# Loading w_in through GpSimd's DMA queue and a q sketch in eight tiles, in a fused sketched-attention and feed-forward kernel

## Chip, cores and metric

The kernel runs on one core of a Trainium2 chip. The metric is the device time of one execution in microseconds (us); where several executions were timed, their median.

## What is computed

Polynomial-sketch attention over 4 batches and 4 heads (1088 positions, head size 32), then a feed-forward layer with a squared ReLU over all 4352 tokens:

```python
def phi(x):
    a = np.einsum('rd,bhsd->bhsr', S1, x)      # r = 8
    b = np.einsum('rd,bhsd->bhsr', S2, x)
    return np.einsum('bhsi,bhsj->bhsij', a, b).reshape(*x.shape[:-1], r * r)
q_p, k_p = phi(q), phi(k)
kv = np.einsum('bhsf,bhsd->bhfd', k_p, v)
z = np.sum(k_p, axis=2)
num = np.einsum('bhsf,bhfd->bhsd', q_p, kv)
den = np.einsum('bhsf,bhf->bhs', q_p, z)[..., None] + 1e-06
x = (num / den).transpose(0, 2, 1, 3).reshape(B * S, H * D)
out = np.maximum(x @ w_in, 0.0) ** 2 @ w_out   # w_in 128 x 2048, w_out 2048 x 128
```

## The kernel before

The feed-forward layer is cut into ten chunks of tokens (256 to 512 columns, `FC`) and each chunk into 16 blocks of 128 hidden columns. One unit is one or two blocks: a matmul of w_in's block with xT (`ffn1`, L597), ReLU (L609 on ScalarE, or L607 on VectorE), square (L620 or L622), and a matmul with w_out's block that adds up in `po` (`ffn2`, L641). w_in's matmuls run on the type float32r, so w_in is loaded as float32 into `w_in32` (`load_wi`, L208, four quarters of 512 columns) and cast by GpSimd into `w_in` (`cast_wi`, L685). The attention of batches 1 to 3 is woven into the feed-forward work by a planner (`_Order`), which lays out all later instructions by estimated costs and due times; the change leaves it as it is.

What the change touches is the prologue, written out by hand, which brings the first 256 columns of xT for batch 0. In order:

- Loads. S1 and a first piece of v (64 KB, token tiles 0 to 3 of partition group 0) go out on ScalarE's queue; S2, two pieces of k, the first 256 columns of q, seven more pieces of v, then w_in and w_out quarters, more q and the next batches go out on SP's queue, one after another (L181 to L213).
- While k is on its way TensorE runs fillers (`keep_warm`, L692) and the little product that spreads S1 and S2 (`sp`, L703; copied to `ss` by ScalarE, L706). GpSimd builds `iden` and `sel`, then from `ss` the q sketch weights `sq` (L721), the replicator `irep` (L728), pads and small weights (L732 to L744).
- k: VectorE transposes k in four groups of token tiles, (0,2), (2,2), (4,3), (7,2) (`a_kT0`, L290); TensorE sketches each token tile with four 128x32 matmuls (`a_kf`, L315); ScalarE copies one half to `kb` (L321); VectorE multiplies the halves to `kp` (`a_kp0`, L331); TensorE adds kp with v and a column of ones to `kvp` (`a_kv0`, L396).
- q: VectorE transposes 256 columns (`a_qT`, L296), TensorE sketches them (`q0`, L756, four matmuls on 64x128 tiles), ScalarE copies one half (`qb0`, L767), VectorE multiplies (`qp0`, L774).
- Then numerator, denominator and normalization: `zb`, `bd`, `zm` on VectorE (L789 to L800), `den` and `num` on TensorE (L816, L821), transposes and a reciprocal on VectorE (L837 to L843), and the product into xT (L844). ScalarE copies kvt and sw (L809, L830), TensorE replicates kvt (L440). One filler (L835) already reads w_in; then the first L597.

An engine works through its instructions in the order written. In `kernel` order TensorE sees all four `a_kf`, both `q0`, then all `a_kv0`; VectorE sees the four `a_kT0`, `a_qT`, then the four `a_kp0`. `kvp` takes a buffer that the second `a_kf` has used, so it follows the second `a_kp0`.

Of the kernel before, what the change touches and what calls it, by code (L numbers as in the profile page):

```python
# [10 lines left out]
F32R = mybir.dt.float32r  # L11
# [3 lines left out]
def _ap(t: bass.AP, p0: int, np_: int, off: int, free):  # L15
    p = list(t.ap)[0]
    return bass.AP(
        t.tensor, t.offset + p0 * p[0] + off, [[p[0], np_]] + [list(d) for d in free]
    )
# [88 lines left out]
def kernel(  # L108
# [11 lines left out]
    nc = tc.nc  # L120

    B, H, S, D = 4, 4, 1088, 32
# [5 lines left out]
    GT, G2, LA = 4, 6, 3.5  # L128
    LU = 4
    KC = [(0, 160), (160, 128)]  # L130
    W0, W1, W3 = 5, 3, 1
    ND, QT, WI, KL, QL = 2, 6.0, (1.0, 1.9), (30.0, 8.0), 4.0


# [10 lines left out]
    mult = mybir.AluOpType.mult  # L145
# [10 lines left out]
    psf = ctx.enter_context(tc.tile_pool(name="psf", bufs=2, space=bass.MemoryType.PSUM))  # L156
# [3 lines left out]
    def sb(name, cols, dt=F32, rows=128):  # L160
        return cpool.tile([rows, cols], dt, tag=name, name=name)
# [6 lines left out]
    vn = [sb("vn0", VC + 32), sb("vn1", VC)]  # L168
    kT, qT = sb("kT", SP), sb("qT", SP)
    xT = sb("xT", B * S + SP - S, F32R)  # L170
    w_in32, w_o, w_in = sb("w_in32", 2048), sb("w_o", 2048), sb("w_in", 2048, F32R)
    s_nat, ss, s2f = sb("s_nat", 32, rows=16), sb("ss", 80), sb("s2f", 32)
    sf, s_T = ss[:, 0:64], ss[:, 64:80]

# [22 lines left out]
    def load_v(eng, b, p, t0=0, t1=NT):  # L197
        n = 32 * ((t1 if p < 3 else min(t1, NT - 2)) - t0)
        eng.dma_start(
            _ap(vn[b % 2], 32 * p, 32, 32 * t0, [[32 * NT, H], [1, n]]),  # L200
            bass.AP(
                v.tensor, v.offset + b * H * S * D + 32 * first(b, t0, p),
                [[G * D, 32], [S * D, H], [1, n]],
            ),
        )

    def load_wi(eng, c):
        eng.dma_start(  # L208
            w_in32[:, 512 * c : 512 * c + 512], moe_w_in[:, 512 * c : 512 * c + 512]
        )  # L210

    def load_wo(eng, c):
        eng.dma_start(  # L213
            _ap(w_o, 0, 128, 512 * c, [[128, 4], [1, 128]]),
            bass.AP(
                moe_w_out.tensor, moe_w_out.offset + c * 512 * 128,
                [[128, 128], [128 * 128, 4], [1, 128]],
            ),
        )
# [2 lines left out]
    nc.sync.dma_start(s_nat[8:16, :], S2[:, :])  # L222
    load_k(nc.sync, 0, 0, 512)
    load_k(nc.sync, 0, 512, S)
    load_v(nc.scalar, 0, 0, 0, 4)
    load_q(nc.sync, 0, 0, 256)
    for t0, t1 in ((0, 4), (4, NT)):
        for p in range(0 if t0 else 1, 4):
            load_v(nc.sync, 0, p, t0, t1)

    zero_a = sb("zero_a", 8)
    nc.scalar.copy(zero_a[:, :], nc.const_aps.tensor(0.0, (128, 8), F32))

    sq, sel = sb("sq", 256), sb("sel", 320, rows=16)
    nc.vector.memset(sel[:, :], 0.0)
    nc.gpsimd.memset(_ap(vn[0], 96, 32, 32 * (NT - 2), [[32 * NT, H], [1, 64]]), 0.0)
    nc.gpsimd.memset(vn[0][:, VC : VC + 32], 1.0)
# [2 lines left out]
    kt0 = sb("kt0", SP)  # L240
# [8 lines left out]
    for i in range(2):  # L249
# [5 lines left out]
    own_h, own_q = sb("own_h", 4), sb("own_q", 2)  # L255
# [3 lines left out]
    nc.gpsimd.tensor_copy(  # L259
        _ap(sel, 0, 16, 64, [[80, 4], [1, 16]]), _ap(iden, 0, 16, 0, [[0, 4], [1, 16]])  # L260
    )
    nc.vector.tensor_reduce(
        out=own_h[:, :], in_=_ap(iden, 0, 128, 0, [[32, 4], [1, 32]]), op=add, axis=AX
    )
# [2 lines left out]
        out=own_f[:, :], in_=_ap(iden, 0, 128, 0, [[8, 16], [1, 8]]), op=add, axis=AX  # L267
# [11 lines left out]
    def banks(t_, x, col, n, k=2):  # L279

        return _ap(t_, 0, 128, 512 * x + col, [[512, k], [1, n]])
# [5 lines left out]
    def a_kT0(t0, n):  # L287
        p = 3 if t0 + n > NT - 2 else 4
        i = 32 * (first(0, t0, 1) - first(0, t0, 0))
        nc.vector.transpose(  # L290
            _ap(kt0, 0, 128, 128 * t0, [[32, p], [128, n], [1, 32]]),
            _ap(kn[0], 0, 128, 32 * first(0, t0, 0), [[i, p], [32, n], [1, 32]]),
        )

    def a_qT(b, i0, n):
        nc.vector.transpose(qT[:, 32 * i0 : 32 * i0 + 32 * n], qn[b % 2][:, 32 * i0 : 32 * i0 + 32 * n])  # L296
# [10 lines left out]
                )  # L307


    def a_kf(t0, n, pool, tag):  # L310
        kf = pool.tile([128, 512], F32, tag=tag, name="kf")
        for t in range(n):
            for c in range(4):
                o = 128 * (t0 + t) + 32 * c
                nc.tensor.matmul(  # L315
                    _ap(kf, 32 * c, 32, 32 * t, [[32 * n, 2], [1, 32]]),
                    kt0[:, o : o + 32],
                    sf,
                )
        kb = wpool.tile([128, 32 * 3], F32, tag="kb", bufs=4, name="kb")  # L320
        nc.scalar.copy(kb[:, 0 : 32 * n], kf[:, 32 * n : 64 * n])  # L321
        st["kf", t0] = kf, kb

    def new_kp(b):

        st[b, "kp"] = wpool.tile([128, 64 * NT * H], F32, tag="kp", name="kp")

    def a_kp0(t0, n):

        kf, kb = st["kf", t0]  # L330
        nc.vector.tensor_tensor(  # L331
            out=_ap(st[0, "kp"], 0, 128, 256 * t0, [[64, 4 * n], [8, 8], [1, 8]]),
            in0=_ap(kf, 0, 128, 0, [[8, 4 * n], [1, 8], [0, 8]]),
            in1=_ap(kb, 0, 128, 0, [[8, 4 * n], [0, 8], [1, 8]]),
            op=mult,
        )
# [344 lines left out]
        nc.vector.tensor_copy(ob[1][:, :], po[1][:, 0:128])  # L681
        store(1)

    def cast_wi(c):
        nc.gpsimd.tensor_copy(  # L685
            w_in[:, 512 * c : 512 * c + 512], w_in32[:, 512 * c : 512 * c + 512]
        )

    def keep_warm(n, cols=512):
        t_ = st["warm"]  # L690
        for _ in range(n):
            nc.tensor.matmul(  # L692
                t_[:, 0:cols],
                nc.const_aps.tensor(1.0, (128, 128), mybir.dt.bfloat16),
                nc.const_aps.tensor(1.0, (128, cols), mybir.dt.bfloat16),
            )
# [8 lines left out]
        )  # L705
    nc.scalar.copy(ss[:, :], sp[:, 0:80])  # L706
    load_q(nc.sync, 0, 256, 640)
    load_wi(nc.sync, 0)
    load_wi(nc.sync, 1)
    load_wi(nc.sync, 2)  # L710
    load_wo(nc.sync, 0)
    load_wo(nc.sync, 1)
    load_wi(nc.sync, 3)
    for c in range(2, 4):
        load_wo(nc.sync, c)
    load_q(nc.sync, 0, 640, S)
    keep_warm(W1)
    a_kT0(0, 2)
    a_kT0(2, 2)
    for x in range(2):  # L720
        nc.gpsimd.tensor_tensor(  # L721
            out=_ap(sq, 0, 128, 128 * x, [[64, 2], [8, 8], [1, 8]]),
            in0=_ap(ss, 0, 128, 72 - 8 * x, [[0, 2]] + [[[0, 8], [1, 8]], [[1, 8], [0, 8]]][x]),
            in1=_ap(own_q, 0, 128, 0, [[1, 2], [0, 8], [0, 8]]),
            op=mult,
        )
    for h in range(H):
        nc.gpsimd.tensor_copy(  # L728
            _ap(irep, 32 * h, 32, 0, [[32, 4], [1, 32]]),
            _ap(iden, 32 * h, 32, 32 * h, [[0, 4], [1, 32]]),  # L730
        )
    nc.gpsimd.memset(_ap(vn[1], 96, 32, 32 * (NT - 2), [[32 * NT, H], [1, 64]]), 0.0)  # L732
    for w in sw:
        nc.gpsimd.memset(w[:, 16:32], 0.0)
# [2 lines left out]
        out=_ap(sfk, 0, 128, 0, [[16, 2], [1, 16]]),  # L737
        in0=_ap(ss, 0, 128, 64, [[0, 2], [1, 16]]),
        in1=_ap(own_q, 0, 128, 0, [[1, 2], [0, 16]]),
        op=mult,  # L740
    )
    nc.gpsimd.memset(kT[:, S:SP], 0.0)
    nc.gpsimd.memset(qT[:, S:SP], 0.0)
    nc.gpsimd.memset(_ap(pd, 0, 128, 8, [[9, 4 * NT], [1, 1]]), 1e-6)  # L744

    a_kT0(4, 3)
    a_kT0(7, 2)
    a_qT(0, 0, 8)


    x0 = att("x0")

    def q0(x):
        for y in range(2):
            r, o = slice(64 * y, 64 * y + 64), 512 * (2 * x + y)
            nc.tensor.matmul(x0[:, o : o + 256], sq[r, 128 * x : 128 * x + 128], qT[r, 0:256])  # L756

    new_kp(0)
    qb0 = wpool.tile([128, 512], F32, tag="qb0", bufs=1, name="qb0")
    qp0 = wpool.tile([128, 512], F32, tag="qp0", bufs=1, name="qp0")  # L760
    a_kf(0, 2, psf, "po")
    a_kf(2, 2, psf, "pg")
    a_kf(4, 3, psf, "po")
    a_kf(7, 2, psf, "pg")
    q0(0)
    q0(1)
    nc.scalar.copy(_ap(qb0, 0, 128, 0, [[256, 2], [1, 256]]), banks(x0, 0, 0, 256))  # L767
    st[0, "kvp"] = psf.tile([128, 512], F32, tag="pg", name="kvp")
    for t0, n in ((0, 2), (2, 2), (4, 3), (7, 2)):
        a_kp0(t0, n)  # L770
        for t in range(t0, t0 + n):
            a_kv0(t)

    nc.vector.tensor_tensor(  # L774
        out=_ap(qp0, 0, 128, 0, [[256, 2], [1, 256]]), in0=banks(x0, 2, 0, 256),
        in1=_ap(qb0, 0, 128, 0, [[256, 2], [1, 256]]), op=mult,
# [7 lines left out]
    bd = sb("bd", 128)  # L784
    own = _ap(own_p, 0, 128, 0, [[0, 2], [1, 2], [0, 32]])

    for c in range(4):
        cast_wi(c)
    nc.vector.tensor_tensor(  # L789
        out=_ap(zb, 0, 128, 1, [[65, 2], [32, 2], [1, 1]]),  # L790
        in0=_ap(st[0, "kvp"], 0, 128, 32, [[64, 2], [0, 2], [1, 1]]),
        in1=_ap(own_p, 0, 128, 0, [[0, 2], [1, 2], [1, 1]]),
        op=mult,
    )
    nc.vector.tensor_tensor(
        out=_ap(bd, 0, 128, 0, [[64, 2], [32, 2], [1, 32]]),
        in0=_ap(st[0, "kvp"], 0, 128, 0, [[64, 2], [0, 2], [1, 32]]),
        in1=own, op=mult,
    )
    nc.vector.tensor_tensor(  # L800
        out=_ap(zm, 0, 128, 0, [[16, 2], [8, 2], [1, 8]]),
        in0=_ap(st[0, "kvp"], 0, 128, 32, [[64, 2], [0, 2], [1, 8]]),
        in1=_ap(own_f, 0, 128, 0, [[0, 2], [8, 2], [1, 8]]),
        op=mult,
# [46 lines left out]
    tu, t = [], 1.2  # L851
# [310 lines left out]
```

## Time and profile before

| | us |
|---|---|
| median of 3 runs | 184.5 (184.16 to 184.61) |
| profiled execution | 184.55 |
| its span, first to last instruction | 182.7 |
| TensorE busy in it | 178.3 |
| ScalarE, VectorE, GpSimd busy | 135.9, 121.8, 39.4 |
| first ffn1 matmul (L597) starts at | 12.95 |

Times in the timelines count from the start of the span. A line of a timeline reads: start, duration, engine, source line, operation, output<-inputs, tile shape on TensorE (rows*columns), operand shape, type, number of merged instructions; in brackets the idle time before it and what ended that. PE is TensorE, DVE VectorE, ACT ScalarE, POOL GpSimd, and a trailing q the DMA issues of an engine. A float32 matmul shows as two records, a float32r one as one. A matmul's duration includes its way through the array, so neighbours overlap; their pace is read from the distance of their starts.

### The profile page before, as it was taken

How to read it: one execution, taken by the hardware profiler on the slowest of the kernel's cores; microseconds unless marked ns; L12 is line 12 of the kernel's file. 1: busy time of each engine (PE TensorE's matmuls, PEld its weight loads, DVE VectorE, ACT ScalarE, POOL GpSimd, SP SyncE). 2: the span in 40 equal slices, each digit the busy share in tenths (PEclk: the TensorE clock that was granted, in tenths of full speed). 3: DMA queues.
4: the chain of work that ended last, by engine and by line, in shares of the span. 5: the costliest groups of instructions: out<-in, count | busy, mean ns of one | idle time of the engine just before them, and what ended most of it. 6: DMA issues, size and time to landing. Idle time of an engine off the chain costs nothing.

```text
span 182.7 us, 3995 instructions
## 1 busy us (share of the span) xinstructions
PE 178.3 (98%) x1529; PEld 105.3 (58%) x1529; DVE 121.8 (67%) x262; ACT 135.9 (74%) x258; POOL 39.4 (22%) x158
## 2 busy tenths in 40 slices
PE   8999999999999999999999999999999999999992
PEld 2768876755645655555455554545555554555792
DVE  3979969999999961799994335996353334333640
ACT  3329679849948886799937778894777777777990
POOL 5544418438300002570008100500000000000000
PEclk9999999999999999999999999999999999999999
DMA  5999990010029700000030200003003000300111
GB/s 150 225 304 341 298 238 17 4 32 0 0 47 238 179 0 4 4 2 0 0 54 14 43 0 5 0 0 59 0 4 57 0 0 5 52 0 0 32 29 29
DMA packets 24610, 11.26 MB, mean 62 GB/s; under 512 B 17936, under 2 KB 23056, under 8 KB 24592
## 3 DMA queue, kind: packets, MB, share of 16 engines
q1 hardware_dynamic: 24272, 10.89, 24.0%
q8 instruction: 12, 0.20, 0.4%
q10 hardware_dynamic: 320, 0.13, 0.3%
q14 instruction: 6, 0.05, 0.1%
HBM read 8.78 MB, written 2.23 MB: 60 GB/s over the span
## 4 chain that ended last, share of the span: by engine, by line
PE 98%; DVE 0%; issue 0%; ACT 0%; ACTq 0%
PE po L641 61%; PE pg L597 18%; PE nd L550 3%; PE po L636 2%; PE warm L692 2%; PE pol L636 2%; PE qc L303 2%; PE nd L414 1%; PE kvp L396 1%; PE kf L315 1%; PE qc L347 1%; PE kvp L414 1%; PE x L756 1%; PE nd L347 0%; PE den L816 0%; PE x L440 0%
## 5 line engine op out<-in xcount | busy, mean ns | idle before, releaser
L641 PE MATMUL po<-g,w_o 128*128 128x512 f32 (+3 forms) x288 | 122.7, 546 | 0.0
L609 ACT ACTIVATE gt<-pg 128x512 f32<-128x512 f32 (+3 forms) x144 | 75.2, 570 | 31.3 <-PE pg L597 30.8
L641 PEld LDWEIGHTS po<-g,w_o 128*128 128x128 f32 x288 | 53.4, 189 | 31.9 <-issue 24.8
L597 PE MATMUL pg<-xT,w_in 128*128 128x512 f32 (+3 forms) x160 | 70.2, 519 | 0.0
L620 ACT ACTIVATE g<-gt 128x512 f32<-128x512 f32 (+2 forms) x102 | 60.7, 623 | 1.6
L622 DVE TENSOR_TENSOR g<-gt 128x512 f32<-128x512 f32 (+3 forms) x43 | 30.0, 699 | 39.5 <-ACT gt L609 38.8
L597 PEld LDWEIGHTS pg<-xT,w_in 128*128 128x128 f32 x160 | 29.1, 190 | 28.6 <-ACT gt L609 11.5
L510 POOL COPY rd<-rc 32x9 f32<-32x9 f32 (+2 forms) x80 | 19.7, 246 | 26.5 <-DVE rc L502 23.3
L456 POOL COPY kv<-kvt 32x64 f32<-32x64 f32 x48 | 12.7, 264 | 44.7 <-DVE kvt L433 42.5
L519 DVE STREAM_SHUFFLE qa<-qc 128x576 f32<-128x576 f32 (+2 forms) x20 | 11.8, 647 | 0.0
L534 DVE TENSOR_TENSOR qp<-qa,qb 128x576 f32<-128x576 f32 (+2 forms) x20 | 10.8, 605 | 0.0
L482 DVE STREAM_TRANSPOSE qt<-qc 128x576 f32<-128x576 f32 (+2 forms) x10 | 5.8, 611 | 6.2 <-PE qc L347 4.4
L367 DVE TENSOR_TENSOR kp<-fs 128x576 f32<-128x576 f32 x12 | 8.7, 741 | 0.0
L645 DVE STREAM_TRANSPOSE oT<-po 128x512 f32<-128x512 f32 (+3 forms) x9 | 5.9, 653 | 2.1 <-PE po L641 2.1
L550 PE MATMUL nd<-qp,kv 32*32 32x288 f32 (+2 forms) x320 | 6.6, 354 | 0.0
L519 DVE STREAM_SHUFFLE qb<-qc 128x576 f32<-128x576 f32 (+2 forms) x10 | 6.1, 649 | 0.0
L567 DVE TENSOR_TENSOR xT<-nd,bc 128x576 fp32r<-128x576 f32 (+2 forms) x10 | 5.6, 594 | 0.6 <-PE nd L550 0.5
L636 PE MATMUL po<-w_o,g 128*128 128x128 f32 x32 | 5.8, 279 | 0.0
L296 DVE STREAM_TRANSPOSE qT<-qn 128x192 f32<-128x192 f32 (+3 forms) x11 | 5.8, 552 | 0.0
L636 PE MATMUL pol<-w_o,g 128*128 128x128 f32 x32 | 5.7, 275 | 0.0
L560 DVE STREAM_TRANSPOSE bc<-rd 128x576 f32<-128x576 f32 (+2 forms) x10 | 5.7, 596 | 0.0
L550 PEld LDWEIGHTS nd<-qp,kv 32*32 32x32 f32 x320 | 2.9, 103 | 3.6 <-issue 2.4
(106 smaller groups left out, 91.2 us busy)
## 6 DMA issues: line engine op xcount, KB each, us to landing
kn<-in_k_dram SPq DMA_DIRECT2D x3, 544.0 KB, 6.9
qn<-in_q_dram SPq DMA_DIRECT2D x3, 544.0 KB, 7.6
vn<-in_v_dram SPq DMA_DIRECT2D x9, 144.0 KB, 6.3
w_in<-in_moe_w_in_dram SPq DMA_DIRECT2D x4, 256.0 KB, 4.8
w_o<-in_moe_w_out_dram SPq DMA_DIRECT2D x4, 256.0 KB, 5.9
out_dram<-oT SPq DMA_DIRECT2D x12, 64.0 KB, 1.9
out_dram<-oT SPq DMA_DIRECT2D x8, 56.0 KB, 1.8
out_dram<-oT SPq DMA_DIRECT2D x8, 48.0 KB, 1.8
```

The source lines that it names most:

```text
L367: nc.vector.tensor_tensor(out=_ap(st[b, "kp"], 0, 128, 64 * NT * h, [[64, NT], [8, 8], [1, 8]]), in0=_ap(fs, 0, 128, o, [[32, NT], [1, 8], ...
L456: nc.gpsimd.tensor_copy(_ap(st[b, "kv"], 32 * c, 32, 64 * h, [[32, E], [1, 32]]), _ap(st["kvt"], 32 * h, 32, 0, [[64, E], [1, 32]]),)
L510: nc.gpsimd.tensor_copy(st[b, "rd", i0][32 * h : 32 * h + 32, n * c : n * c + n], st["rc"][32 * c : 32 * c + 32, n * h : n * h + n],)
L519: nc.vector.stream_shuffle(in_=banks(st[b, "qc", i0], 2 * x, 0, m), out=_ap(st[b, which, i0], 0, 128, 2 * m * x, [[m, 2], [1, m]]), mask=m ...
L534: nc.vector.tensor_tensor(out=st[b, "qp", i0, e][:, r], in0=st[b, f"qa{e}", i0][:, r], in1=st[b, "qb", i0][:, r], op=mult,)
L550: nc.tensor.matmul(nd[32 * h : 32 * h + 32, 512 * c : 512 * c + m], kv[r, o : o + 32], qp[r, m * h : m * h + m], start=(e == 0), stop=(e = ...
L597: nc.tensor.matmul(st["pg", u][:, n * i : n * i + n], w_in[:, 128 * (d0 + i) : 128 * (d0 + i) + 128], xT[:, c0 : c0 + n],)
L609: nc.scalar.activation(gt[:, 0:w], st["pg", u][:, 0:w], Relu)
L620: nc.scalar.activation(to, of, Square)
L622: nc.vector.tensor_tensor(out=to, in0=of, in1=of, op=mult)
L636: nc.tensor.matmul(po[x // 128][:, 0:128], g[:, x : x + 128], w, start=(d == 0), stop=(d == NB - 1),)
L641: nc.tensor.matmul(po[0][:, 0:n], w, g, start=(d == 0), stop=(d == NB - 1))
```

## The change

The first two pieces of v and all of w_in are issued by GpSimd. The load of w_in writes the float32r tile itself, so `w_in32` and the four casts are gone; two quarters go out behind the copies of `irep`, two behind the pads. SP issues w_out and q without w_in between. `sq` loses the multiplication by a mask, and the q sketch becomes eight matmuls on 32x64 tiles; its copy to `qb0` becomes two copies that each swap the partition halves. The first `a_kp0` now stands ahead of `a_qT` on VectorE; the last `a_kf` uses two 128x64 matmuls per token tile instead of four 128x32; of the three fillers after `sp` the last is 384 columns instead of 512.

```diff
-    W0, W1, W3 = 5, 3, 1
+    W0, W1, W3 = 5, 2, 1
...
-    def load_wi(eng, c):
-        eng.dma_start(
-            w_in32[:, 512 * c : 512 * c + 512], moe_w_in[:, 512 * c : 512 * c + 512]
+    def load_wi(c):
+        nc.gpsimd.dma_start(
+            w_in[:, 512 * c : 512 * c + 512], moe_w_in[:, 512 * c : 512 * c + 512]
         )
...
-    load_v(nc.scalar, 0, 0, 0, 4)
     load_q(nc.sync, 0, 0, 256)
     for t0, t1 in ((0, 4), (4, NT)):
-        for p in range(0 if t0 else 1, 4):
+        for p in range(0 if t0 else 2, 4):
             load_v(nc.sync, 0, p, t0, t1)
...
+    for p in range(2):
+        load_v(nc.gpsimd, 0, p, 0, 4)
...
-    def a_kf(t0, n, pool, tag):
+    def a_kf(t0, n, pool, tag, w=32):
         kf = pool.tile([128, 512], F32, tag=tag, name="kf")
         for t in range(n):
-            for c in range(4):
-                o = 128 * (t0 + t) + 32 * c
+            for c in range(0, 128, w):
+                o = 128 * (t0 + t) + c
                 nc.tensor.matmul(
-                    _ap(kf, 32 * c, 32, 32 * t, [[32 * n, 2], [1, 32]]),
-                    kt0[:, o : o + 32],
+                    _ap(kf, c, w, 32 * t, [[32 * n, 2], [1, 32]]),
+                    kt0[:, o : o + w],
                     sf,
                 )
...
     load_q(nc.sync, 0, 256, 640)
-    load_wi(nc.sync, 0)
-    load_wi(nc.sync, 1)
-    load_wi(nc.sync, 2)
-    load_wo(nc.sync, 0)
-    load_wo(nc.sync, 1)
-    load_wi(nc.sync, 3)
-    for c in range(2, 4):
+    for c in range(4):
         load_wo(nc.sync, c)
     load_q(nc.sync, 0, 640, S)
     keep_warm(W1)
+    keep_warm(1, 384)
...
     for x in range(2):
-        nc.gpsimd.tensor_tensor(
-            out=_ap(sq, 0, 128, 128 * x, [[64, 2], [8, 8], [1, 8]]),
-            in0=_ap(ss, 0, 128, 72 - 8 * x, [[0, 2]] + [[[0, 8], [1, 8]], [[1, 8], [0, 8]]][x]),
-            in1=_ap(own_q, 0, 128, 0, [[1, 2], [0, 8], [0, 8]]),
-            op=mult,
+        nc.gpsimd.tensor_copy(
+            _ap(sq, 0, 128, 64 * x, [[8, 8], [1, 8]]),
+            _ap(ss, 0, 128, 72 - 8 * x, [[[0, 8], [1, 8]], [[1, 8], [0, 8]]][x]),
         )
...
+    load_wi(0)
+    load_wi(1)
     nc.gpsimd.memset(_ap(vn[1], 96, 32, 32 * (NT - 2), [[32 * NT, H], [1, 64]]), 0.0)
...
     nc.gpsimd.memset(_ap(pd, 0, 128, 8, [[9, 4 * NT], [1, 1]]), 1e-6)
+    load_wi(2)
+    load_wi(3)
...
     a_kT0(7, 2)
-    a_qT(0, 0, 8)
...
     def q0(x):
-        for y in range(2):
-            r, o = slice(64 * y, 64 * y + 64), 512 * (2 * x + y)
-            nc.tensor.matmul(x0[:, o : o + 256], sq[r, 128 * x : 128 * x + 128], qT[r, 0:256])
+        for h in range(H):
+            r, o, p = slice(32 * h, 32 * h + 32), 512 * (2 * x + h // 2), 64 * ((h + 1 - x) % 2)
+            nc.tensor.matmul(
+                x0[p : p + 64, o : o + 256], sq[r, 64 * x : 64 * x + 64], qT[r, 0:256]
+            )
...
     a_kf(0, 2, psf, "po")
+    a_kp0(0, 2)
+    a_qT(0, 0, 8)
     a_kf(2, 2, psf, "pg")
     a_kf(4, 3, psf, "po")
-    a_kf(7, 2, psf, "pg")
+    a_kf(7, 2, psf, "pg", 64)
     q0(0)
     q0(1)
-    nc.scalar.copy(_ap(qb0, 0, 128, 0, [[256, 2], [1, 256]]), banks(x0, 0, 0, 256))
+    for i in range(2):
+        nc.scalar.copy(
+            _ap(qb0, 64 * i, 64, 0, [[256, 2], [1, 256]]),
+            _ap(x0, 64 - 64 * i, 64, 0, [[512, 2], [1, 256]]),
+        )
...
-    for c in range(4):
-        cast_wi(c)
```

More of the change, by code (lines that the diff above doesn't have):

```diff
@@ L170 @@
     xT = sb("xT", B * S + SP - S, F32R)
-    w_in32, w_o, w_in = sb("w_in32", 2048), sb("w_o", 2048), sb("w_in", 2048, F32R)
+    w_o, w_in = sb("w_o", 2048), sb("w_in", 2048, F32R)
     s_nat, ss, s2f = sb("s_nat", 32, rows=16), sb("ss", 80), sb("s2f", 32)
@@ L232 @@
     nc.scalar.copy(zero_a[:, :], nc.const_aps.tensor(0.0, (128, 8), F32))
-    sq, sel = sb("sq", 256), sb("sel", 320, rows=16)
+    sq, sel = sb("sq", 128), sb("sel", 320, rows=16)
     nc.vector.memset(sel[:, :], 0.0)
@@ L682, in f_last @@
         store(1)
[L684 to L687, printed above, removed]
     def keep_warm(n, cols=512):
@@ L744 @@
     nc.gpsimd.memset(_ap(pd, 0, 128, 8, [[9, 4 * NT], [1, 1]]), 1e-6)
+    load_wi(2)
+    load_wi(3)
     a_kT0(4, 3)
     a_kT0(7, 2)
-    a_qT(0, 0, 8)
     x0 = att("x0")
     def q0(x):
-        for y in range(2):
-            r, o = slice(64 * y, 64 * y + 64), 512 * (2 * x + y)
-            nc.tensor.matmul(x0[:, o : o + 256], sq[r, 128 * x : 128 * x + 128], qT[r, 0:256])
-    new_kp(0)
+        for h in range(H):
[3 more added lines that the diff above has]
+            )
     qb0 = wpool.tile([128, 512], F32, tag="qb0", bufs=1, name="qb0")
     qp0 = wpool.tile([128, 512], F32, tag="qp0", bufs=1, name="qp0")
+    new_kp(0)
     a_kf(0, 2, psf, "po")
+    a_kp0(0, 2)
+    a_qT(0, 0, 8)
     a_kf(2, 2, psf, "pg")
     a_kf(4, 3, psf, "po")
-    a_kf(7, 2, psf, "pg")
+    a_kf(7, 2, psf, "pg", 64)
     q0(0)
     q0(1)
-    nc.scalar.copy(_ap(qb0, 0, 128, 0, [[256, 2], [1, 256]]), banks(x0, 0, 0, 256))
+    for i in range(2):
[3 more added lines that the diff above has]
+        )
     st[0, "kvp"] = psf.tile([128, 512], F32, tag="pg", name="kvp")
     for t0, n in ((0, 2), (2, 2), (4, 3), (7, 2)):
-        a_kp0(t0, n)
+        if t0:
+            a_kp0(t0, n)
         for t in range(t0, t0 + n):
```

## The prediction

> **What bounds the kernel now.** I read the chain of the work that ended last first, then each engine's timeline over the first 18 us, then the waits of that stretch.
>
> ```profile
> PE 98%; DVE 0%; issue 0%; ACT 0%; ACTq 0%
> PE po L641 61%; PE pg L597 18%; PE nd L550 3%; PE po L636 2%; PE warm L692 2%; PE pol L636 2%; PE qc L303 2%; PE nd L414 1%; PE kvp L396 1%; PE kf L315 1%; PE qc L347 1%; PE kvp L414 1%; PE x L756 1%; PE nd L347 0%; PE den L816 0%; PE x L440 0%
> ```
>
> Almost everything is TensorE, most of it the feed-forward matmuls (L641, L597). From 15.9 us to the end they follow each other without a pause that another engine sets, and nothing in the change touches them. So only the stretch before can move the end, and it moves it one to one: what counts is when the first L597 starts (12.95 us) and how long the filling after it, 13 to 16 us, takes. TensorE's timeline there:
>
> ```profile
> 4.80 2.16 PE L315 MATMUL kf<-ss,kt 128*32 128x64 f32 x72
> 6.89 1.14 PE L756 MATMUL x<-qT,sq 64*128 64x256 f32 x8
> 7.96 2.32 PE L396 MATMUL kvp<-vn,kp 128*64 128x64 f32 x72
> ...
> 12.61 0.51 PE L835 MATMUL warm<-w_in 128*128 128x512 f32 x1
> 12.95 0.69 PE L597 MATMUL pg<-xT,w_in 128*128 128x256 f32 x4
> 13.57 0.45 PE L303 MATMUL qc<-qT,sw 32*32 32x96 f32 x32
> 14.01 0.47 PE L597 MATMUL pg<-xT,w_in 128*128 128x256 f32 x2
> ```
>
> L396 starts right behind the q sketch (L756) and runs at an even pace. VectorE shows what stands before and after:
>
> ```profile
> 4.20 0.77 DVE L290 STREAM_TRANSPOSE kt<-kn 128x256 f32<-128x256 f32 x2 [1.61 <-DMA kn<-in_k_dram]
> 5.17 0.84 DVE L290 STREAM_TRANSPOSE kt<-kn 128x384 f32<-128x384 f32 x2 [0.21 <-DMA kn<-in_k_dram]
> 5.94 0.40 DVE L296 STREAM_TRANSPOSE qT<-qn 128x256 f32<-128x256 f32 x1
> 6.26 2.71 DVE L331 TENSOR_TENSOR kp<-kf,kb 128x512 f32<-128x512 f32 x4
> 8.90 0.68 DVE L774 TENSOR_TENSOR qp<-x,qb 128x512 f32<-128x512 f32 x1
> 10.32 0.17 DVE L789 TENSOR_TENSOR zb<-kvp,own_p 128x4 f32<-128x4 f32 x1 [0.75 <-PE kvp L396]
> ```
>
> It waits twice: 0.21 us for the second piece of k, and 0.75 us for L396. So the path is: second piece of k, transposes, q sketch, kvp, then a fixed chain to xT and the first L597. GpSimd's casts, which vanish, look costly but are on no path:
>
> ```profile
> 10.70 0.61 POOL L685 CAST w_in<-w_in 128x512 fp32r<-128x512 f32 x1 [3.52 <-DMA w_in<-in_moe_w_in_dram]
> 11.65 1.26 POOL L685 CAST w_in<-w_in 128x512 fp32r<-128x512 f32 x2 [0.34 <-DMA w_in<-in_moe_w_in_dram]
> 15.00 0.61 POOL L685 CAST w_in<-w_in 128x512 fp32r<-128x512 f32 x1 [2.09 <-DMA w_in<-in_moe_w_in_dram]
> ```
>
> Quarters 0 to 3 of w_in are first used at 12.61, 14.01, 15.56 and 17.65 us (L597 runs through the 16 column blocks in order); the casts end at 11.31, 12.27, 12.91 and 15.61.
>
> **The change part by part.**
>
> *q sketch, later but shorter.* VectorE now does the first kp product before qT. That product takes a slot of 0.58 us (it starts at 6.26, the next at 6.84), so qT ends at 6.34 + 0.58 = 6.92 instead of 6.34; its place in the row of products is the same, so the later ones stay. TensorE sees a transpose 0.16 us after its end (first kt 4.64, first kf 4.80), so the sketch starts at 7.08 instead of 6.89: **+0.19**. Its length: before, 8 records on 64x128 tiles, two at a time, four rounds of 256 columns. Rounds start 0.21 us apart (7.21, 7.43, 7.64), that is 0.83 ns a column, so four rounds are 0.85 of the 1.14 us and 0.29 is start and drain. The nearest row with eight tiles is L347, 64x32, 32 records in 0.78 us: two rounds of 160 columns and two of 128 are 0.48, the rest 0.30. The same rest, so eight tiles do run at once. The new sketch has 16 records on eight tiles: two rounds, 0.43 + 0.30 = 0.73 us: **-0.41**. Together it ends 0.2 us earlier, and kvp with it: **-0.2**. Lower end: no eightfold overlap, -0 in length, so +0.19. Upper end: L396 can't start before the second kp product is read out of its buffer (ends 7.51, so 7.67 against 7.96): -0.29. I take -0.2, from the row that has the same number of tiles. Behind it the third product (8.38) must be there for kvp's record 32 (at 0.029 us each, 8.7 us) and the fourth (8.98) for record 56 (9.4 us); both are, barely.
>
> The Trainium skill (TensorEngine Tiling (Array Packing), Key Properties) says that tiles work independently, but that a change of the tiling mode drains the array, and the change adds one such switch by its 128x64 tiles in the last kf. By that rule the last kf's saving is eaten; the sum stays.
>
> *Last kf in 64-column tiles, 128 warm columns fewer.* Half the records (8 for 16), and a quarter of a 0.41 us filler. Both end before the sketch, which now waits for qT until 7.08 while kf is done by about 6.95: **0**, covered by that wait.
>
> *v's first two pieces to GpSimd.* The piece that ACT issued at 1.37 (64 KB, 3.1 us to landing) ran beside the two pieces of k (544 KB). At the 272 GB/s of the window 3.4 to 6.8 us, 64 KB are 0.24 us of all 16 engines. Gone from there, k's second piece lands up to 0.21 us earlier for VectorE (the idle time before 5.17), or not at all if GpSimd's pieces, issued at 2.4, come in just then. Ends 0 and -0.21; I take the middle, **-0.1**. The pieces themselves land by about 6.5 (2.4, two issues, 3.1 us), and kvp reads them at 7.7: cover 1.2 us.
>
> *qb0 in two copies on ACT.* 0.59 us each, from about 7.85: done at 9.05, so VectorE's qp0 starts 0.15 later than at 8.90 but has 0.75 us of idle time behind it: **0**.
>
> *sq as plain copies, casts gone.* sq is ready by 5 us, needed at 7.08: **0**. The last cast lies over VectorE's pd (L488, 0.59 us for 96 columns), which gets quicker by some 0.3 us (0.25 for 128 columns at 25.99), but TensorE never waits for that chain between 16 and 22 us: **0**.
>
> *w_in through GpSimd.* The trace has no DMA issue on GpSimd and none that converts. Its price on the engine, c: the nearest rows are ACT's issue, 0.35 us, and SP's, 0.43; the longest of SP's, 1.34, was held up by the queue. I take 0.5, near the undisturbed ones, and keep 1.34 for the range. Work between: sq and irep 1.9 us, the pads 1.4. Then the quarters are issued from 5.7, 6.2, 8.1 and 8.6 and land, at the 4.8 us of the old rows under load, at 10.5, 11.0, 12.9 and 13.4, against 12.3, 13.7, 15.3 and 17.3 needed (today's first uses less 0.3): **0**, cover 1.8 us or more. What queues behind on GpSimd: the pads of sw (read by ACT at 11.96) and the rd copies (16.42), both with 2 us to spare. SP loses five issues of 0.47 us, so w_o and the next batch come earlier; nobody waits for them: **0**.
>
> The Trainium skill (DMA: Bandwidth & Descriptors, Latency and other measured facts) puts the first byte at about 1 us for GpSimd's path and 0.6 for SP's and ACT's. With c = 1 the third quarter would land at 14.5 instead of 12.9: the sum would still be the same, with the cover down to 0.8 us.
>
> *Sum:* +0.19 - 0.41 - 0.1 = -0.3 us. The profiled execution took 184.55 us (span 182.7, 1.85 around it, which I leave), 0.05 above the median of 184.5; from the median the forecast is **184.2 us**.
>
> **The rivals.**
>
> *Everything that holds kvp goes.* The whole 0.21 of k, kvp at its earliest (7.67 - 0.21 = 7.46, against 7.96: -0.5), and 0.05 to 0.1 where VectorE's chain to xT no longer runs beside a cast (bc, L843, took 0.45 for 256 columns, qT 0.40). For it: VectorE and kvp are both tight, and both ends are given by rows. Against: all bounds must be met together. -0.6: **183.9**.
>
> *GpSimd's issue is dear (slower).* The third quarter lands at 10.5 + 4c (four issues, 2.4 start, 3.3 work, 4.8 landing; from c = 0.7 on GpSimd no longer waits for ss), needed at 15.3: it decides from c = 1.2 us. Above, L597 of column block 8 stalls and every 0.1 us of c costs 0.4; at 1.34 that leaves 184.8, at c = 1.6 it is 1.6 - 0.3 = 1.3 slower, **185.8**. A converting transfer that takes longer than 4.8 us under load does the same. For: no row of its price; against: all issue rows but the held-up ones are below 0.6.
>
> *It doesn't do what it says.* The sketch's tiles take turns and GpSimd's v pieces meet k's second piece: +0.19, **184.7**.
>
> *TensorE's clock steps up later.* Matmuls of kf start 27 ns apart at 4.8 us (16 in 0.40) and 14 ns apart at 6.7, so the array runs at half pace until about 6.5 although the page grants 1.0 throughout. If less filler let that step slip past kvp, its 72 records would take 53 ns each instead of 29: +1.7, with the sketch +2: **186.2**. Against: 0.1 us of filler in 6.
>
> The Trainium skill (TensorE: Matmul & The Clock Gate, Part 1) has the clock go up after one busy free-running window of about 3.4 us; that fits the step at 6.5, and by it a slip would cost one more such window.
>
> **How the numbers follow.** Forecast 0.48, everything goes 0.24, dear issue 0.17, tiles and v in the way 0.07, clock 0.04. About 0.3% (0.55 us) is what a measurement of this kernel can tell from no change. Only the second case passes it below (its sum -0.6, with a little from the forecast's upper end: 0.25); dear issue and clock pass it above, 0.21; the rest, 0.54, lies within. The range: below, 183.7 leaves out about 0.07 of the second case; above, 185.4 takes in the dear issue up to c = 1.5 and leaves out about 0.12. The likeliest case alone runs from 184.0 (both upper ends, -0.5) to 184.7 (+0.2).
>
> **What would show it.** L756 as 16 records on 32x64, starting near 7.1 and taking near 0.73; L396 starting near 7.65 instead of 7.96; VectorE's wait before the second kt group below 0.21; the first L597 near 12.65, and no wait of L835 or L597 for a DMA of w_in. On GpSimd, the gap of each DMA issue is c. It is wrong if L597 pauses at 14.0, 15.6 or 17.7, if kf or L396 run at twice their pace's spacing, or if the time around the span grows from 1.85 because a queue of another kind is in use.

## The result, and the profile after

The changed kernel takes 186.72 us in the median of 6 executions (185.47 to 188.06); the kernel before, on the same chip, 184.2. The ratio is 1.012, 95% interval 1.0083 to 1.0157: **slower by 1.2%**. The forecast was 184.2 us in a range of 183.7 to 185.4, so the time lies outside the range. Each of the two kernels was profiled twice, since one profile of each had a peculiarity of its own:

| profiled executions, us | before | before, again | after | after, again |
|---|---|---|---|---|
| time | 184.55 | 184.18 | 187.34 | 186.27 |
| q sketch starts | 6.89 | 6.58 | 6.87 | 6.86 |
| kvp (L396, now L397) starts | 7.96 | 7.64 | 7.49 | 7.49 |
| first ffn1 matmul starts | 12.95 | 12.64 | 13.66 | 12.48 |
| from there to the start of the last matmul | 166.22 | 166.21 | 167.89 | 168.02 |
| from there to the end of the span | 3.56 | 3.54 | 4.00 | 3.99 |

Read the two "again" columns against each other: the first ffn1 matmul comes 0.16 us earlier, as meant, and 2.26 us are lost behind it: 1.81 in the stretch that the prediction called untouched and 0.45 after the last matmul. That leaves 2.1 us net. The timeline of TensorE after the change, first profile, the prologue:

```profile
4.71 1.73 PE L316 MATMUL kf<-ss,kt 128*32 128x64 f32 x64
6.87 0.69 PE L748 MATMUL x<-qT,sq 32*64 32x256 f32 x16 [0.43 <-DVE qT L297]
7.49 1.15 PE L397 MATMUL kvp<-vn,kp 128*64 128x64 f32 x32
9.60 1.39 PE L397 MATMUL kvp<-vn,kp 128*64 128x64 f32 x40 [0.97 <-DVE qp L775]
...
13.32 0.49 PE L834 MATMUL warm<-w_in 128*128 128x512 f32 x1
13.66 0.69 PE L598 MATMUL pg<-xT,w_in 128*128 128x256 f32 x4
```

The sketch has its 16 records and takes 0.69 us for 1.14; kvp starts 0.47 earlier than in the first profile of before, but stops for 0.97 us after 32 records. The line puts that down to VectorE's qp (L775), which ended at 9.54. But kvp doesn't need qp: in the second profile it passes the same record at 8.47, over 1 us before qp ends. What came last is the last piece of v on SP's queue. Its landings on the 16 DMA engines are done at 7.46 in the median and at 9.36 on the last engine (before: 7.36 and 7.66), and TensorE's wait instruction for that piece goes through at 9.39. In the second profile the piece is done at 8.16, the wait goes through at 8.19, and kvp doesn't stop. VectorE, first profile:

```profile
5.67 0.69 DVE L332 TENSOR_TENSOR kp<-kf,kb 128x512 f32<-128x512 f32 x1
6.28 0.44 DVE L297 STREAM_TRANSPOSE qT<-qn 128x256 f32<-128x256 f32 x1
6.64 2.12 DVE L332 TENSOR_TENSOR kp<-kf,kb 128x512 f32<-128x512 f32 x3
8.85 0.69 DVE L775 TENSOR_TENSOR qp<-x,qb 128x512 f32<-128x512 f32 x1
11.03 0.17 DVE L788 TENSOR_TENSOR zb<-kvp,own_p 128x4 f32<-128x4 f32 x1 [1.48 <-PE kvp L397]
```

The products have no gap between them; all the waiting has moved to zb, behind kvp. What both profiles of the changed kernel share lies at 22 to 25 us, in TensorE's timeline, here of the first and then of the second:

```profile
22.80 0.81 PE L642 MATMUL po<-g,w_o 128*128 128x256 f32 x3
25.20 0.38 PE L642 MATMUL po<-g,w_o 128*128 128x256 f32 x1 [1.59 <-issue]
25.23 0.53 PE L598 MATMUL pg<-xT,w_in 128*128 128x384 f32 x1
```

```profile
22.08 0.81 PE L642 MATMUL po<-g,w_o 128*128 128x256 f32 x3
24.15 0.38 PE L642 MATMUL po<-g,w_o 128*128 128x256 f32 x1 [1.26 <-issue]
```

The second profile has one more such pause, a short one:

```profile
13.10 0.38 PE L304 MATMUL qc<-qT,sw 32*32 32x96 f32 x12
13.74 0.42 PE L304 MATMUL qc<-qT,sw 32*32 32x96 f32 x20 [0.26 <-issue]
```

"issue" means that TensorE waited for nothing that the profile shows. What it waited for stands in the list of DMA packets. The queues of the page after:

```profile
q1 hardware_dynamic: 23552, 9.77, 22.1%
q0 software_dynamic: 640, 1.18, 2.1%
q8 instruction: 12, 0.20, 0.5%
```

q0 is GpSimd's queue, new with the change. q8, by the count, carries TensorE's **own instructions**: each of its 12 packets is a block of 16 KB, 256 instructions. Counted from the start of the program (matmuls, weight loads and waits), the long pause stands exactly after TensorE's instruction 705 in both profiles, and the packet that brings the block behind it runs from 22.61 to 23.71 in the first and from 21.27 to 22.50 in the second, while TensorE reaches the end of what it has at 23.24 and 22.52. Before, that packet ran from 17.38 to 18.64 for a need at 22.81. The short pause of the second profile stands after instruction 449, exactly one block earlier; that packet had run from 11.30 to 12.18. From one start to the next the two pauses cost about 1.4 and 0.5 us, which covers the 1.81.

The trace doesn't show when a block is asked for. In these four profiles none of the first seven packets ran before TensorE had passed the last-but-one block's end (instruction 449 for block 705), while three of the last five ran 0.2 to 2.9 us before it. I take that moment as the request, as an estimate that serves to compare the same block between runs: before, block 705 waited 3.8 and 3.1 us for its turn, after the change 8.2 and 8.0.

### The profile page after: what moved, and what is told of

Same layout as the page of the kernel before. It is cut to its first block, busy times and chain, and to the rows that moved or that the text cites. A ratio compares the mean times of both kernels' runs of the same rounds, so it can differ in the third digit from the quotient of the medians.

```text
span 185.5 us, 3997 instructions
## 1 busy us (share of the span) xinstructions
PE 177.7 (96%) x1529; PEld 104.7 (56%) x1529; DVE 121.7 (66%) x262; ACT 136.4 (74%) x259; POOL 40.1 (22%) x160
## 4 chain that ended last, share of the span: by engine, by line
PE 95%; DVE 1%; issue 1%; ACT 1%; ACTq 0%
PE po L642 60%; PE pg L598 18%; PE nd L551 3%; PE po L637 2%; PE pol L637 2%; PE warm L688 2%; PE qc L304 2%; PE nd L415 1%; PE qc L348 1%; PE kvp L397 1%; PE kvp L415 1%; ACT qb L764 1%; PE x L748 0%; PE nd L348 0%; DVE qp L775 0%
## 5 line engine op out<-in xcount | busy, mean ns | idle before, releaser
L598 PE MATMUL pg<-xT,w_in 128*128 128x512 f32 (+3 forms) x160 | 70.2, 520 | 0.0
L598 PEld LDWEIGHTS pg<-xT,w_in 128*128 128x128 f32 x160 | 29.1, 190 | 30.2 <-ACT gt L610 11.8
```

What stands on the lines that cost most here:

```text
L598: nc.tensor.matmul(st["pg", u][:, n * i : n * i + n], w_in[:, 128 * (d0 + i) : 128 * (d0 + i) + 128], xT[:, c0 : c0 + n],)
```

## The theories and the experiments

The expectations name theories by letters. A: w_in on GpSimd's queue takes turns with SP's transfers and delays them. B: it is v's two pieces on GpSimd. D: it is the conversion to float32r. E: a queue of GpSimd's kind is what hurts; F: any second queue would. G: TensorE lacks its next block of instructions; H: it lacks data.

### The parts alone

The changed kernel without the w_in part:

```diff
-    load_wi(0)
-    load_wi(1)
...
-    load_wi(2)
-    load_wi(3)
...
+    load_wi(nc.sync, 0)
+    load_wi(nc.sync, 1)
+    load_wi(nc.sync, 2)
...
+    for c in range(4):
+        cast_wi(c)
```

> The changed kernel, but w_in back on SP's queue in its old place, with its float32 tile and GpSimd's casts; v's first two pieces stay on GpSimd and the sketch stays in eight tiles. Theory A (w_in on GpSimd's queue takes turns with SP's queue on the DMA engines, so that the last piece of v and TensorE's instruction load come late): both pauses go, L396 starts near 7.5 and runs through, the first L597 comes near 12.6, 0.25 to 0.35 us under the kernel before (183.9). Theory B (the v pieces on GpSimd are what holds the last v piece): L396 still pauses near 8.6, the first L597 comes no earlier than 13.0, time 184.5 or more.

Measured: 184.38, ratio 1.0009 (0.9993 to 1.0026); block 705 waits 2.0 us and no matmul pauses. The kernel before with the sketch part alone (tiles, copies, order on VectorE, fillers):

```diff
+    a_kp0(0, 2)
+    a_qT(0, 0, 8)
...
-    a_kf(7, 2, psf, "pg")
+    a_kf(7, 2, psf, "pg", 64)
```

> The kernel before with the sketch part alone (eight tiles, kp ahead of qT, two copies to qb0, last kf in 64 columns, fewer filler columns, sq as copies); all loads as before. By the prediction's own step: kvp 0.2 us earlier, the first L597 near 12.75, time 0.2 under the kernel before (184.0). If the sketch itself were the fault: L396 pauses or starts later than 7.96, time over 184.5.

Measured: 184.31, ratio 1.0007 (0.9991 to 1.0022). TensorE's timeline of the kernel before, second profile, then of this one:

```profile
4.81 1.84 PE L315 MATMUL kf<-ss,kt 128*32 128x64 f32 x72
6.58 1.13 PE L756 MATMUL x<-qT,sq 64*128 64x256 f32 x8
7.64 2.32 PE L396 MATMUL kvp<-vn,kp 128*64 128x64 f32 x72
...
12.64 0.71 PE L597 MATMUL pg<-xT,w_in 128*128 128x256 f32 x4
```

```profile
6.99 0.69 PE L754 MATMUL x<-qT,sq 32*64 32x256 f32 x16 [0.18 <-DVE qT L296]
7.62 2.32 PE L396 MATMUL kvp<-vn,kp 128*64 128x64 f32 x72
...
12.61 0.68 PE L597 MATMUL pg<-xT,w_in 128*128 128x256 f32 x4
```

The sketch is 0.44 us shorter and starts 0.41 us later: nothing is left. In the profile that the prediction was made from, TensorE ran kf at half pace until about 6.5 us, in the second one of before only until about 5.5, so there the sketch starts right behind qT, at 6.58, and kvp is held by the second kp product. Next, the kernel before with the w_in part alone, and with the v part alone:

```diff
-    load_wi(nc.sync, 0)
-    load_wi(nc.sync, 1)
-    load_wi(nc.sync, 2)
...
+    load_wi(0)
+    load_wi(1)
...
```

> The kernel before with w_in through GpSimd's queue alone (no casts, SP without w_in); v and sketch as before. Theory A: L396, which starts at 7.96, pauses for the last piece of v that lands after 8.7, and TensorE pauses once more between 20 and 27 us in the middle of two records of one matmul; time 186 to 188, and it varies by 1 us or more. Theory B: no pause, time within 0.3 of the kernel before.

```diff
-    load_v(nc.scalar, 0, 0, 0, 4)
...
+    for p in range(2):
+        load_v(nc.gpsimd, 0, p, 0, 4)
```

> The kernel before with v's first two pieces on GpSimd alone; w_in on SP, sketch as before. Theory A: k's second piece lands 0.2 to 0.4 us earlier (4.76 after the change, 5.15 before), nothing pauses, time 0.1 to 0.4 under the kernel before. Theory B: the last v piece lands after 8.7, L396 pauses, time over the kernel before by 0.3 or more.

Measured: w_in alone 185.0, ratio 1.0035 (1.0022 to 1.0047); v alone 184.81, ratio 1.0024 (1.0014 to 1.0034). With w_in alone block 705 waits 3.8 us, no longer than in the first profile of before, and no matmul pauses for instructions. In its profile the stretch from the first ffn1 matmul to the last matmul is 166.12 us, as before; 0.3 us are lost behind the last matmul, and the first ffn1 matmul starts at 13.31. There kf ran at half pace to its end, with starts still 27 ns apart at 7.0 us, and one profile doesn't tell how much of that late start belongs to the change. VectorE with v alone:

```profile
6.74 0.45 DVE L297 STREAM_TRANSPOSE qT<-qn 128x256 f32<-128x256 f32 x1 [1.28 <-DMA qn<-in_q_dram]
```

k's second piece no longer makes VectorE wait, but q's first piece does: it has landed at 4.91 on half the engines and at 6.71 on the last. The three parts alone give +0.1, +0.7 and +0.4 us by their ratios, 1.2 together; the change costs 2.2. So I joined the sketch and w_in, with v as before:

> Sketch part and w_in through GpSimd, with v's pieces as before (ScalarE and SP). The parts alone cost 0 (sketch) and 0.65 (w_in). If the pause near 23 us needs only w_in on GpSimd beside a SP queue that is 2 us ahead: 185.5 to 186.5, with the pause. If it needs v on GpSimd too: 184.7 to 185.1, no pause.

Measured: 185.94 (184.7 to 187.26), ratio 1.0078 (1.0045 to 1.0111), and block 705 waits 5.7 us. The profile is of the fastest of the ten executions; it has no long pause (stretch 166.29 us). A is supported: with the sketch and v in place, taking w_in off GpSimd restores the time. B holds only for a part. That w_in seems to cost more with the quicker sketch (1.4 us) than alone (0.7) was not expected; the two intervals just touch, and the runs don't explain it.

### Which property of the transfers

The changed kernel with plain float32 transfers on GpSimd's queue, and the casts of before:

```diff
-            w_in[:, 512 * c : 512 * c + 512], moe_w_in[:, 512 * c : 512 * c + 512]
+            w_in32[:, 512 * c : 512 * c + 512], moe_w_in[:, 512 * c : 512 * c + 512]
...
+    for c in range(4):
+        cast_wi(c)
```

> The changed kernel, but GpSimd's queue loads w_in as plain float32 into its own tile and GpSimd casts it as before; issue order and times of the queue as changed. Theory D (the conversion within the transfer is what is slow and lags): the late landings go, the first L597 comes near 12.6, time 184 to 184.5. Theory A or E (it is GpSimd's queue, whatever it carries): as the changed kernel, 185.5 to 187.5.

Measured: 185.58, ratio 1.0054 (1.0036 to 1.0072); block 705 waits 5.2 us. So a good part of the loss is there without a conversion, and D isn't the whole. But this loss isn't of one kind with that of the changed kernel: block 705 causes no pause in the profile, and L598 waits 0.34 and 0.58 us for casts, which the changed kernel doesn't have. Whether the conversion adds the rest stays open: the two intervals hardly separate (1.0072 and 1.0083), and a packet of 2 KB took 98 ns converting, 84 ns on SP's queue before, in the median, with the same mean of 109 ns.

v's two pieces on ScalarE's queue, on the kernel before:

```diff
-    load_v(nc.scalar, 0, 0, 0, 4)
...
+    for p in range(2):
+        load_v(nc.scalar, 0, p, 0, 4)
```

> The kernel before, with v's first two pieces issued by ScalarE behind its first copy (about 2.9 and 3.3 us) in place of GpSimd (2.3 and 3.0); SP has six pieces of v as after the change. Theory E (transfers that GpSimd issues make one or two of the 16 DMA engines fall behind, for all queues): no lag, q's first piece lands by 5.6 (6.7 with GpSimd's issue), time 184.0 to 184.3, that is 0.5 to 0.8 under the run with GpSimd's v alone. Theory F (any second queue beside SP's at that time does it, or SP's new order): as with GpSimd's v alone, 184.8.

Measured: 184.68, ratio 1.0014 (1.0002 to 1.0025), and no clear difference from GpSimd's 184.81. ScalarE issued them at 1.45 and 1.82, earlier than meant, so this one doesn't settle E against F. It leans to F: q's first piece has again landed late on the last engine, at 6.61 (6.71 with GpSimd's issue), with no transfer of GpSimd at all. The changed kernel, with w_in's quarters plain on ScalarE's queue:

```diff
+    load_wi(nc.scalar, 0)
+    load_wi(nc.scalar, 1)
     a_kf(4, 3, psf, "po")
...
```

> The changed kernel with w_in as plain float32 on ScalarE's queue, issued near 6.2 and 8.7 us, and cast by GpSimd as before; v's first two pieces stay on GpSimd. Theory E (it is GpSimd's queue that holds up the others): late landings and pause go, 184.2 to 184.6. Theory F (any second queue that takes turns with SP's): as with GpSimd and no conversion, 185.6 or more.

Measured: 191.32, ratio 1.0378 (1.0338 to 1.0418). ScalarE's timeline:

```profile
9.44 5.04 ACTq L208 DMA_DIRECT2D w_in<-in_moe_w_in_dram  x2
14.58 0.27 ACT L815 COPY kvt<-kvp 128x128 f32<-128x128 f32 x1 [5.08 <-DMA w_o<-in_moe_w_out_dram]
```

The last two issues hold ScalarE for 5.04 us, and the copies that TensorE needs stand behind them (L441 waits 2.78 us). Then the clock adds to it: right behind this wait TensorE's granted clock is 0.51 from 15 to 17 us and 0.50 from there to 25 us, and in every other profile it is 1.00 at that time. The first ffn1 matmul comes at 16.28, 3.6 us later than in the second profile of before, and the stretch behind it is 4.4 us longer. That is a price of its own. TensorE's blocks, though, wait only 2.6 us here, both 449 and 705, against 4.4 and 8.2 in the changed kernel. So for the blocks E is favoured over F, not proved, since the requests fall at other moments. As for room, the Trainium skill (DMA: Bandwidth & Descriptors, Issuing engines are not separate DMA queues) says that all issuers end on the same 16 DMA engines and interleave. The trace agrees: from 14 to 18 us the engines' share is 1.08 before and 1.09 after, full both times.

### Instructions or data

Two edits of the changed kernel that move TensorE's count of instructions or SP's traffic. First, the same filler columns in eleven short matmuls, eight matmuls more:

```diff
-    keep_warm(W1)
-    keep_warm(1, 384)
+    keep_warm(11, 128)
```

> The changed kernel with its 1408 columns of filler after sp cut in eleven pieces of 128 instead of 512, 512 and 384: 16 more TensorE instructions in the same time. Theory G (the pause near 23 us is TensorE waiting for its next block of instructions, which is loaded late): the pause again comes after the 705th instruction, and so 16 instructions earlier in the program, at another matmul; time as the changed kernel, 185.5 to 187.5. Theory H (that matmul waits for data, w_out, w_in or a buffer): the pause stays at the same matmul, the second w_out product behind the first 384-column product.

Measured: 188.43, from executions of 185.66, 187.76, 189.1 and 190.06 us, too far apart for a verdict on the time (ratio 1.0244, 1.0184 to 1.0304). The profile is of the fastest. Second, SP's next batch of k held back until VectorE is past xT, by a write into its tile:

```diff
+    nc.vector.memset(kn[1][:, 0:8], 0.0)
     a_qT(0, 14, 6)
```

> The changed kernel, with the next batch's loads on SP held until xT's first columns are written (a small write of VectorE to the tile of the next k, near 13 us), where SP otherwise issues them from 10.2. If SP's early traffic beside GpSimd's is what holds up TensorE's instruction load and the late quarters: that load comes near 17 us as before, the pause near 23 goes, time 184.3 to 185. If GpSimd's transfers alone do it: pause and time as the changed kernel. The held k lands near 20.5, before its use at 21.5, give or take 0.5.

Measured: 186.33, ratio 1.0106 (1.0077 to 1.0136), as the changed kernel. TensorE's timelines of the two:

```profile
36.41 0.49 PE L551 MATMUL nd<-qp,kv 32*32 32x128 f32 x31
37.52 0.29 PE L551 MATMUL nd<-qp,kv 32*32 32x128 f32 x1 [0.61 <-issue]
```

```profile
13.13 0.38 PE L304 MATMUL qc<-qT,sw 32*32 32x96 f32 x12
14.82 0.42 PE L304 MATMUL qc<-qT,sw 32*32 32x96 f32 x20 [1.30 <-issue]
```

The pauses now stand elsewhere, in the middle of rows of like matmuls whose data are there, but again exactly at a block's end: after instruction 1217 (packet 34.95 to 36.07, need 36.64) and after 449 (packet 12.57 to 13.53, need 13.27). 449, 705 and 1217 are each 193 plus a multiple of 256. The run with short fillers missed its sign as it was put: block 705 was in at 19.58 there, before its need at 20.96, and no pause shows. Its pause at 1217 isn't the queue's doing either: that block waited only 0.2 us from the request at 34.79, but the 256 instructions in between, most of them rows of short matmuls, were through in 1.9 us. The second run still pauses at 705 too, for 0.25 us. H falls: with the count or the timing moved, pauses turn up at three different matmuls, and each one stands at a block's end. So G is shown for these pauses, though not for everything that the change costs. The second run also clears SP's early next batch: with its issue held from 10.43 to 12.46, near the 12.79 of before, block 705 still waits 8.4 us. In all these cases the matmul resumes 1.3 to 1.7 us behind the packet's end, which the trace doesn't explain; it is why a packet that ends before its need, as at 36.07, can still be late.

Both kernels were profiled once more:

> The kernel before once more, for a second profile. If the first profile was a slow one (184.55 against a median of 184.33), the first L597 comes near 12.7 instead of 12.95, and TensorE needs the same 166.2 us from there to its last matmul.

> The changed kernel once more, for a second profile. Theory A and E: the pauses vary with which landings lag; the first L597 again at 12.6 to 13.8, and either a pause of 1 to 2 us in the middle of a matmul near 23 us, with TensorE's instruction load late before it, or none and then a time near 185.5. A fixed cost of the change would show the same two pauses of the same size.

Measured: 184.18 and 186.27, the columns above. The pause at instruction 705 came again (1.26 us), and a shorter one at 449 (0.26 us); that of kvp didn't come again.

### How much of w_in

Open was whether it is the transfers outstanding at the request, the amount, or the early quarters. The changed kernel with half of w_in on SP:

```diff
+    load_wi(nc.sync, 0)
+    load_wi(nc.sync, 1)
     for c in range(4):
         load_wo(nc.sync, c)
...
+    load_wi(nc.gpsimd, 2)
+    load_wi(nc.gpsimd, 3)
```

> The changed kernel with w_in's quarters 0 and 1 back on SP's queue with their casts; only quarters 2 and 3 go through GpSimd, in their late place behind the pads (issued near 8 us, landed near 15.5). Block 705 of TensorE's instructions is asked for near 13.3 us. Theory 1 (what counts is GpSimd traffic that is outstanding when the block is asked for): the load waits about 8 us as in the changed kernel, starts at 20 or later, the matmuls pause near 22.5, and the time is 185.5 to 186.7. Theory 2 (what counts is the amount that GpSimd carries in all): half the excess, a load near 18, no pause in most executions, 184.9 to 185.4. Theory 3 (the early quarters, issued near 5.5, are what pushes everything back): the load starts near 16 as in the kernel before, 184.3.

> The changed kernel with only quarters 0 and 1 of w_in through GpSimd, in their early place behind the copies of irep (issued near 5.5 us, landed near 12.5); quarters 2 and 3 go on SP's queue behind two quarters of w_out, with casts. Theory 1 (outstanding GpSimd traffic when block 705 is asked for): all of GpSimd's traffic has landed by 13.3, so the load waits 2 to 4 us and starts at 15.5 to 17.5 as without GpSimd, no pause, 184.2 to 184.6. Theory 2 (amount): the same as with the late half, a load near 18, 184.9 to 185.4. Theory 3 (the early quarters): load at 20 or later, a pause near 22.5, 185.5 to 186.7, and the last piece of v later than 8.5 in some executions.

Measured: late half 185.52, ratio 1.0053 (1.0026 to 1.0081), block 705 waits 4.7 us; early half (the same edit with quarters 0 and 1 on GpSimd) 185.99, ratio 1.0072 (1.0038 to 1.0106), waits 5.2 us. None and all stand at 2.0 and 8.0. Theories 1 and 3 fall: either half does about the same. Theory 2, the amount, fits best, though both halves cost more than the 184.9 to 185.4 that it gave. In the profiles each half lost at another place: the late one waited 0.73 us for a cast of w_in at 14.27 and 0.48 us for w_out at 15.24, the early one 1.04 us in kvp for v's last piece (landed at 9.64 on the last engine). Neither pauses at block 705. So the runs show that time goes to whatever comes late, v's last piece, an instruction block, w_out or a cast, and that this differs from profile to profile; they don't show one common cause of the lateness.

Last, a version without any second queue: the sketch part, qT again ahead of kp, v's first piece on SP.

```diff
-    load_v(nc.scalar, 0, 0, 0, 4)
...
-        for p in range(0 if t0 else 1, 4):
+        for p in range(4):
```

> No transfer on GpSimd at all: the sketch part alone, with VectorE's transpose of q back ahead of the first kp product, and with the first piece of v moved from ScalarE's queue to SP's, so that all eight pieces follow k and q there. If what the runs so far showed adds up: k's second piece lands some 0.2 us earlier since no piece of v runs beside it, the sketch starts right behind qT near 6.5, kvp is held by the second kp product near 7.4 instead of 7.64, the first feed-forward matmul starts near 12.4, and the time is 184.0 to 184.2 with no pause after 13 us. Rival: v's first pieces now land last and hold kvp (issued 0.5 us later than in the kernel before, landing near 7.9), or q's first piece lags on a few engines as with v's pieces elsewhere: 184.4 to 184.8.

Measured: 184.97 (184.2 to 186.02), ratio 1.0036 (1.0011 to 1.0062). It missed: kvp starts at 7.41, 0.23 earlier, but takes 2.56 instead of 2.32 us, so zb starts at 10.01 as before. It stops before the same record as in the changed kernel, and again for v: the product that it needs ended at 8.22, v's last piece landed at 8.45 on the last engine, TensorE's wait for it went through at 8.48. That is the rival that the expectation named. The executions scatter. No version here beats the kernel before.

## Why the prediction was wrong, point by point

- **"w_in through GpSimd ... 0, cover 1.8 us or more": the step that failed.** The price of the issue was nearly right: 0.55 to 0.59 us of GpSimd (0.71 the first; 0.5 was taken), and the dear-issue rival's 1.2 is far off. The landing was mis-sized: a quarter took 4.8 to 7.4 us (median 6.7) instead of the 4.8 of the old rows. In the first profile the quarters land by 10.26, 12.48, 14.89 and 15.86 for uses at 13.32, 14.72, 16.18 and 18.30. So the cover was thinner than said (in the second profile the third quarter has 0.14 us), but no matmul waited for w_in in either. The step asked only whether w_in itself is late. It left out everyone else on the 16 DMA engines: v's last piece, and TensorE's instruction blocks, a row of the page before (q8) with 0.4% of the engines' time. The blocks' price was 1.7 and 1.8 us in the stretch behind the first ffn1 matmul; v's piece cost 1.0 more in kvp in one profile.
- **"From 15.9 us to the end ... nothing in the change touches them"** failed with it: TensorE still has to fetch its program there, and the change reached those transfers.
- **The time after the last matmul** was left as it is, and it grew by 0.45 us. There, in the trace's records, SyncE checks a list of semaphores, two at a time and 0.06 us apart, and GpSimd clears them; the kernel before has five such checks, the changed one eight, which makes some 0.2 of the 0.45 us. Over all 17 profiles the stretch is 3.54 to 3.56 us with no GpSimd transfer, 3.74 to 3.75 with two, 3.87 with four and 3.99 to 4.00 with six. The 0.45 us are a fifth of the loss; the 0.2 and 0.3 us of two and four transfers are about half of what v and w_in each cost alone. The prediction named growth around the span as a sign; it came inside it, at its end.
- **Sketch, -0.2:** length as forecast (0.69 for 0.73), start 6.87 for 7.08. The net was 0, because the base was an execution in which kf ran slowly for 1 us longer: that the first profile's 6.89 and 7.96 stood for every execution was an assumption that failed. The bound that the prediction itself gave, the second kp product, is what holds kvp in the other profile of before.
- **v to GpSimd, -0.1:** k's second piece did land earlier (last engine 4.76 for 5.15). But alone the part cost 0.4 us, half of it at the end of the program, the rest, in the profile, by q's late piece. In the version without w_in (1.0009) that piece landed at 5.50 and nothing waited for it, though GpSimd carries the same pieces of v there; so it isn't late each time.
- **qb0, sq, casts, kf tiles: 0**, all right: no wait for any of them appears in the changed kernel's profiles.
- **The clock rival** was right in kind: the step moves from execution to execution, even of one kernel (5.5 and 6.5 us before). In the 17 profiles it comes anywhere from before 4.7 us (plain transfers on GpSimd's queue) to after 7.0 (w_in alone). It never slipped past the sketch, which took 0.69 or 1.13 to 1.14 us in all of them.

The Trainium skill (Runtime: NRT & Kernel Launch, Instruction fetch mechanics) says that instructions come in 16 KiB blocks by a DMA queue of the engine's own and that crossing a block is "mostly hidden". The trace agrees with the first half (256 instructions to a block) and with the second for the kernel before (block 705 is in 4.2 us before it is needed); in the changed kernel the crossing costs the 1.59 us of the line above.

What stays open: which DMA engines lag and why, since the records carry no engine number, and why an instruction packet of 16 KB waits 8 us while packets of data go by. Open is also how the loss splits in the executions that weren't profiled. Some of them show a granted clock of 0.989 to 0.991 in the mean and are among the longest of their version (188.06 of the changed kernel, 190.06 with short fillers, 187.99 with the late half); whether a pause cost them the clock too, as in the version on ScalarE's queue, no trace shows.

## What to carry to other kernels

A transfer moved to another queue is not paid for when its own data are in time: list everything else that lands in the same stretch, the engines' own instruction blocks among it, and how much room each has. When TensorE pauses on "issue" in the middle of a row of like matmuls, count its instructions: pauses that lie a multiple of 256 apart (here 193 plus such a multiple) point to late blocks. And each transfer of GpSimd added about 0.08 us at the end of the program, so a handful of small ones can eat the gain that they were made for.

## What the runs showed of the hardware that was not expected

- GpSimd's transfers take no longer to land than SP's here: in the version without w_in, v's pieces issued at 2.29 by GpSimd and at 2.58 by SP both have landed 2.9 us later (median engine).
- In saturated stretches the last of the 16 engines lands up to 3 us behind the median (second profile of before, next batch's k: 17.95 and 21.08; first: 17.75 and 19.41), also with no transfer of GpSimd at all.
- Executions of one program differ in when TensorE's pace doubles (the kernel before: about 5.5 or 6.5 us). A step that ends near such a point can't be priced from one profile.
